# Transposed first-layer inputs kept in DRAM between two uses, in a fused state-space mixer and MLP

## The chip, the cores and the metric

The kernel runs on one core of a Trainium2 chip. The metric is device time in microseconds (us), the median of five runs. A profile, which is one execution taken by the hardware profiler, gives the times of the single instructions.

## The reference

```python
def _A_ref(x, Lambda_re, Lambda_im, B_re, B_im, C_re, C_im, log_dt, Dskip):
    Lam = Lambda_re + 1j * Lambda_im
    ...
    dt = jnp.exp(log_dt)
    Lam_bar = jnp.exp(dt * Lam)
    B_bar = ((Lam_bar - 1.0) / Lam)[:, None] * Bmat
    Bu = jnp.einsum("bld,pd->blp", x + 0j, B_bar)
    ...
    for t in range(L):
        h = Lam_bar[None, :] * h + Bu[:, t, :]
        hs.append(h)
    hseq = jnp.stack(hs, 1)
    return 2.0 * jnp.einsum("blp,dp->bld", hseq, Cmat).real + x * Dskip[None, None, :]

def _B_ref(x, w1, b1, w2, b2):
    y = _layernorm(x, axis=-1)
    h = _gelu(jnp.einsum("bsd,df->bsf", y, w1) + b1)
    return jnp.einsum("bsf,fd->bsd", h, w2) + b2

x = A_x
g = _sigmoid((x * gate_w).sum(-1, keepdims=True))
a = _A_ref(x, A_Lambda_re, ..., A_Dskip)
b = _B_ref(x, B_w1, B_b1, B_w2, B_b2)
return g * a + (1 - g) * b
```

x has 2048 tokens of 1024 channels in bfloat16, the state space has 1024 complex states, and the hidden layer of the MLP has 3584 columns.

## The kernel before

Every large product is done with seven block products instead of eight (Strassen's scheme in Winograd's form, class `SG`): a 2x2 split of both factors, four sums of the stationary blocks (S1 to S4) and four of the moving blocks (T1 to T4), and seven calls p1 to p7, each a run of matmuls with 512 moving columns recorded by the helper `mm` (line 839 where a bank is begun, line 841 where it is added to). Sums of blocks are VectorE subtractions and additions by the helper `dve_tt`, all with line 893.

The program runs through these stages on TensorE: the input product of the state space (the u blocks), then the list

```python
blocks = [("m", 0, 0), ("b", 0, 0), ("m", 0, 1), ("b", 0, 1), ("m", 1, 1), ("b", 1, 1), ("m", 1, 0), ("b", 1, 0), ("y", 0, 0)]
```

Here m(Fh, c) is the first MLP layer for half Fh of the hidden columns and half c of the tokens (c = 0 is the first 1024), seven groups of 256 hidden columns; b(Fh, c) is the second layer for the same halves, four groups of 256 tokens; y is the output product of the state space, eight groups. In m the moving factor is the transposed normalised x, which lies in an SBUF region `XN` of seven tiles, 128 partitions by 2048 two-byte values (512 KB) each. Tiles 0, 1 and 2 hold B11, B21 and B22; tiles 3, 4 and 5 hold T1, T2 and T3; tile 6 first holds B12, and T4 overwrites it. There is one such region, so m(0,0) uses the first tokens, m(0,1) and m(1,1) the second, and m(1,0) the first again.

`xn_load(c, q)` fills tiles 0, 6, 1 and 2 with four transposing DMAs (line 1217) from `scr_xn`, the normalised rows in DRAM, and `xn_sums` makes the other four tiles' contents with four subtractions of 2048 columns on VectorE, in the two later cases during the third group of the b block before the m block. Both happen three times: for c = 0 ahead of m(0,0), for c = 1 in b(0,0) and for c = 0 once more in b(1,1). The region is overwritten in place, so a load waits for the matmuls that last read its tile.

The state-space recurrence is VectorE work of sixteen units (`ssm`): load of u from `scr_u` (line 1147, on SP), multiplications and combinations (lines 1160 and 1163), scans (line 1174), and a store of the states to `scr_h` from POOL (line 1192). It runs between the sums and the evictions of the MLP stages: `cadd` (line 1297) in m, line 1379 in b. The first-layer weights come by line 1248 (raw, with four sums of 512 columns on VectorE after them, and kept in DRAM by line 1263 for the second hidden half) or by line 1245 (with their sums, from `scr_w1`). The second-layer weights come by line 1320, four pieces in the first groups of m(0,0) and of m(1,1), followed by four sums of 3584 columns. Second-layer results go to `scr_ac` from POOL (line 1386, and line 1388 adding in DRAM).

The order on each engine is not written by hand. Every operation is a task of class `Graph`, with a modelled duration, a priority and dependencies drawn from the buffers that it reads and writes. `_schedule_once` runs a list schedule of all tasks, and `emit` writes each engine's instructions in that fixed order with the semaphore waits. In a priority tuple the smaller goes first: MLP work has 10.0 and a position in TensorE's sequence (`q`), the recurrence has 50.0 and fills in. A DMA that follows another waits for it on the issuing engine, and an engine takes its list strictly in order. `extra` adds dependencies; `pe_last` is the matmul run that was recorded last. Plain and transposing loads are issued by SP, stores by POOL:

```python
def dma(self, prio, emit, nbytes, sem, reads=(), writes=(), name="", xpose=False, extra=(), ndma=1, bw=None, thr=False, q="sp"):
    if bw is None:
        bw = DMAT_BW if xpose else DMA_BW
    idur = {"sp": SP_ISSUE, "act": ACT_ISSUE, "pool": POOL_ISSUE}[q] * ndma
    ...
```

The main loop takes the groups in order; in iteration x of an m block it records p7 of the group before, p5, p6, p2 and p3 of this one, and then p4 of the group before.

Of the kernel before, what the change touches and what calls it, by code (L numbers as in the profile page):

```python
# [8 lines left out]
BF16 = mybir.dt.bfloat16  # L9
# [410 lines left out]
def build(nc, A_x, A_Lambda_re, A_Lambda_im, A_B_re, A_B_im, A_C_re, A_C_im, A_log_dt, A_Dskip,  # L420
          B_x, B_w1, B_b1, B_w2, B_b2, gate_w, out, stats=None):
# [22 lines left out]
    g = Graph()  # L444
    es = ExitStack()
    with es:
# [25 lines left out]
        AR = Arena(sb("ar", [128, ASZ // 2], BF16), ASZ)  # L472
# [7 lines left out]
        XN = AR.alloc(28672)  # L480
# [17 lines left out]
        B = g.buf  # L498
# [21 lines left out]
        def ssem(name, k, final=False):  # L520
            key = (name, k)
            if key not in slot_sems:
                slot_sems[key] = sem("d_%s%d" % (name, k), dram=final)
                if final and name in ("out", "outl"):
                    final_sems.append(slot_sems[key])
            return slot_sems[key]
# [57 lines left out]
        def bcast(ap, off, name):  # L584
# [11 lines left out]
              reads=[b_ones], writes=[b_ident], name="ident")  # L596
# [88 lines left out]
        def last_pe():  # L685
# [11 lines left out]
              reads=[b_stg, b_ident], writes=[b_ps[bk0]], name="cst_T", extra=last_pe())  # L697
# [3 lines left out]
              reads=[b_ones], writes=[b_stg], name="signs").slack = 4.0  # L701
# [3 lines left out]
              reads=[b_ps[bk0]], writes=[bc(n) for n in stage_names] + [b_ps[bk0]], name="cst_copy")  # L705
# [80 lines left out]
        for k in range(LT):  # L786
            n = 1 << k
# [15 lines left out]
        for p0 in range(0, PT, 4):  # L803
# [4 lines left out]
                  reads=[e1i], writes=[vt], name="tab_s%d" % p0)  # L808
# [16 lines left out]
        seq = [0]  # L825
        pb = [1.0]
        pe_last = []
# [380 lines left out]
            return AR.v(XN + i * 4096 + dt * 1024, [(1, 512)], FP16 if i > 2 else BF16)  # L1208


        def xn_load(c, q):
            for th in range(2):
                for dh in range(2):
                    i = (0, 1)[dh] if th == 0 else (6, 2)[dh]
                    o = AR.v(XN + i * 4096, [(512, 4), (1, 512)])
                    r0 = c * 1024 + th * 512
                    g.dma((10.0, q - 30, dh), lambda e, o=o, r0=r0, dh=dh: e.dma_start_transpose(out=o.ap, in_=XNS[r0:r0 + 512, dh * 512:(dh + 1) * 512]), 512 * 512 * 2,
                          ssem("xnT", i), reads=[b_xns[r0 // 128 + k] for k in range(4)], writes=[o], name="xnT%d.%d.%d" % (c, th, dh), xpose=True)
            xs_todo.append(c)
# [219 lines left out]
        def y_load(yi, ts=(0, 1), state=True):  # L1439

            qb = YORD[yi]
            o = AR.v(H0[yi], [(1, 2 * UE)])
            if state:
                g.dma((52.0, yi), lambda e: e.dma_start(out=o.ap, in_=HS[qb]), 2 * UE * 128 * 2, ssem("hg", yi), reads=[b_hs[pg][qb] for pg in range(PG)], writes=[o], name="hg%d" % yi,
                  extra=pe_last if yi > 2 else ())
            if yi == 0 and state:
                g.dma((51.0, 0), lambda e: e.dma_start(out=v_db.ap, in_=bass.AP(A_Dskip.tensor, A_Dskip.offset, [[0, 128], [1, D]])), 128 * D * 2, sem("d_dskb"), writes=[v_db], name="dskb")
            for t in ts:
                n = 2 * yi + t
                k = 2 * qb + t  # L1450
                av = AR.v(AV[n % 8], [(1, D)], F32)
                xi = 0 if n < 1 else 1 + n % 4
                xv = AR.v(XV[xi], [(1, D)])
                g.dma((52.0, n), lambda e, av=av, k=k: e.dma_start(out=av.ap, in_=ACS[k]), 128 * D * 4, ssem("yac", n % 8), reads=[b_acs[k]], writes=[av], name="acl%d" % k)
                g.dma((52.0, n), lambda e, xv=xv, k=k: e.dma_start(out=xv.ap, in_=x2[k * 128:(k + 1) * 128, :]), 128 * D * 2, ssem("yx", xi), writes=[xv], name="yx%d" % k)
                g.add("dve", c_tt16(D), (49.0, n), lambda e, xv=xv: e.tensor_tensor(xv.ap, xv.ap, v_db.ap, ALU.mult), reads=[xv, v_db], writes=[xv], name="xd%d" % k)
                g.add("dve", c_dve(D), (49.0, n, 1), lambda e, xv=xv, av=av, k=k: e.scalar_tensor_tensor(av.ap, xv.ap, C("G", k), av.ap, ALU.mult, ALU.add),
                      reads=[xv, av, bc("G")], writes=[av], name="xa%d" % k)
# [72 lines left out]
        for n, it in enumerate(flat):  # L1531
            bi, x = it
            kind, Fh, c = blocks[bi]
            last_of_block = (n + 1 == len(flat)) or flat[n + 1][0] != bi
            nit = None if n + 1 == len(flat) else flat[n + 1]
            if (kind, Fh, c, x) == ("b", 1, 0, 3):
                y_load(0, ())
            if (kind, x) == ("y", 0):
                y_load(2)
            if cur is None:  # L1540
                cur = make(it)
                cur.p1()

            if prev is not None:
                prev.p7()
            if kind == "b" and x + 1 < 4:
                prep_s((bi, x + 1), seq[0] + 4)
            if kind == "b" and Fh == 1 and c == 0 and x == 3:
                y_prep(0, seq[0] + 4)
            if kind == "y":  # L1550
                if x + 1 < 8:
                    y_prep(x + 1, seq[0] + 4)
            if kind == "b" and x == 0:

                cur.p2()
            if not early5:
                cur.p5()
            early5 = False
            cur.p6()
            if kind != "b" or x > 0:  # L1560
                cur.p2()
            if nit is None:
                cur.p7()
            cur.p3()
            if prev is not None:
                prev.p4()
                if kind == "y" and 1 <= x and x + 2 < 8:
                    y_load(x + 2)
                if kind == "m":
                    w2_step(seq[0] + 19)  # L1570
                if kind == "m" and 0 < x < 4:
                    w1_next(18)
                elif kind == "m":
                    w1_due[0] += x > 0
            if kind == "b":
                if w1_due[0]:
                    w1_due[0] -= 1
                    w1_next(20, list(pe_last))
                if x == XSG:
                    xn_sums(seq[0] + 20)  # L1580
            if n == 0:
                def em_b2(e):
                    return [e.dma_start(out=AR.v(B2B, [(1, D)], npart=1).ap, in_=bass.AP(B_b2.tensor, B_b2.offset, [[0, 1], [1, D]])),
                            e.dma_start(out=AR.v(B2B + 1024, [(1, 512)], npart=1, p0=1).ap, in_=bass.AP(B_b2.tensor, B_b2.offset, [[0, 1], [1, 512]]))]
                g.add("pool", 0.8, (39.0, 0), lambda e: e.memset(v_b2.ap, 0.0), writes=[v_b2], name="b2z")
                g.dma((40.0, 0), em_b2, 4096, sem("d_b2b"), writes=[v_b2l, v_b2r], name="b2b", ndma=2)
                w2_load(0)
                for pg in range(PG):
                    for q in range(NQ):
                        ssm(pg, q)  # L1590
            prev, cur = cur, pend
            pend = None
            if last_of_block:
                if nit is None:
                    prev.p4()
                else:
                    nk = blocks[nit[0]][0]
                    if nk == "b":
                        prep = True
                        b0 = None  # L1600

                        cur = make(nit)
                        prev.p7()
                        cur.p1()
                        prev.p4()
                        w1_due[0] += 1
                        prep_s(nit, seq[0])
                        pend = make((nit[0], nit[1] + 1))
                        pend.p1()
                    else:  # L1610
                        cur = make(nit)
                        prev.p7()
                        cur.p1()
                        cur.p5()
                        early5 = True
                        prev.p4()
                        if nk == "y":
                            y_load(0, (0, 1), False)
                            y_load(1)
                    prev = None  # L1620
                if (kind, Fh, c) == ("m", 1, 0):
                    ct_load(seq[0] + 20)

                if kind == "m":
                    if (Fh, c) == (0, 0):
                        xn_load(1, seq[0] + 20)
                    elif (Fh, c) == (1, 1):
                        xn_load(0, seq[0] + 20)
                elif (Fh, c) == (0, 1):
                    w2_load(1)  # L1630

# [42 lines left out]
```

## Time and profile before

| | |
|---|---|
| median of five runs | 568.03 us (565.0 to 570.68) |
| profiled execution | 566.27 us |
| its span, first to last instruction | 564.5 us |
| granted TensorE clock, mean | 0.996 |
| TensorE matmul busy | 548.5 us (97%), 2569 matmuls |
| VectorE busy | 519.8 us (92%) |
| ScalarE busy | 279.4 us (50%) |
| POOL busy | 96.3 us (17%) |
| DMA traffic | 125.32 MB, mean 222 GB/s |
| transposing loads from `scr_xn` (line 1217) | 12, median 5.4 us from issue to landing |
| stores to `scr_h` (line 1192), 512 KB each | 16, median 5.6 us, 2.9 to 12.3 |

The span starts with the first instruction, and all positions in time count from there. Busy time is the time in which an engine ran compute instructions; issuing a DMA is not counted as busy for SP. "DMA share" in a window is the mean busy share of the core's 16 DMA engines (it can read a little over 1.00 at the edges of a window). In a list of waits, a line names the engine that stood still, its tile and line, then the instruction that released it, the sum of such waits, their number and the longest.

### The profile page before, as it was taken

How to read it: one execution, taken by the hardware profiler on the slowest of the kernel's cores; microseconds unless marked ns; L12 is line 12 of the kernel's file. 1: busy time of each engine (PE TensorE's matmuls, PEld its weight loads, DVE VectorE, ACT ScalarE, POOL GpSimd, SP SyncE). 2: the span in 40 equal slices, each digit the busy share in tenths (PEclk: the TensorE clock that was granted, in tenths of full speed). 3: DMA queues.
4: the chain of work that ended last, by engine and by line, in shares of the span. 5: the costliest groups of instructions: out<-in, count | busy, mean ns of one | idle time of the engine just before them, and what ended most of it. 6: DMA issues, size and time to landing. Idle time of an engine off the chain costs nothing.

```text
span 564.5 us, 7433 instructions
## 1 busy us (share of the span) xinstructions
PE 548.5 (97%) x2569; PEld 251.7 (45%) x2617; DVE 519.8 (92%) x893; ACT 279.4 (50%) x465; POOL 96.3 (17%) x155
## 2 busy tenths in 40 slices
PE   6999999999999999999989999999999999999995
PEld 5444444444444444444434444444444444444442
DVE  4899999999999999999999999999998995999852
ACT  3969989677652346752236763246763231111110
POOL 0226736620001110001110101220001210000100
PEclk9999999999999999999999999999999999999998
DMA  9995999749774463305988895999778699978501
GB/s 280 237 310 133 284 299 270 262 130 295 218 157 162 175 224 111 113 37 164 322 322 296 287 326 148 228 200 268 261 179 188 114 304 348 393 258 297 188 37 56
DMA packets 122035, 125.32 MB, mean 222 GB/s; under 512 B 70532, under 2 KB 99717, under 8 KB 120974
## 3 DMA queue, kind: packets, MB, share of 16 engines
q1 hardware_dynamic: 108852, 76.97, 47.9%
q0 software_dynamic: 13008, 47.87, 27.1%
q8 instruction: 20, 0.33, 0.2%
q14 instruction: 17, 0.14, 0.1%
q10 hardware_dynamic: 138, 0.02, 0.0%
HBM read 60.73 MB, written 48.38 MB: 193 GB/s over the span
## 4 chain that ended last, share of the span: by engine, by line
PE 82%; DVE 11%; issue 2%; DMA 2%; ACT 1%; POOL 0%; SPq 0%; DVEq 0%
PE ps L841 56%; PE ps L839 25%; DVE ar L893 2%; DVE ar L1174 2%; DMA scr_u<-ar 1%; DVE ar L1160 1%; DVE ar L1019 1%; DVE ar L979 1%; DVE ar L974 1%; PE ps L665 1%; DMA ar<-in_A_B_re_dram 1%; PE ps L1044 1%; DVE ar L820 1%; DVE ar L822 0%; DVE ar L1163 0%
## 5 line engine op out<-in xcount | busy, mean ns | idle before, releaser
L841 PE MATMUL ps<-ar 128*128 128x512 f16 (+1 forms) x1684 | 390.4, 379 | 4.3 <-DVE ar L1379 1.4
L841 PEld LDWEIGHTS ps<-ar 128*128 128x128 f16 (+1 forms) x1720 | 167.7, 98 | 207.0 <-DVE ar L1379 1.9
L839 PE MATMUL ps<-ar 128*128 128x512 bf16 (+1 forms) x744 | 182.8, 380 | 0.6 <-DVE cst L704 0.3
L893 DVE TENSOR_TENSOR ar<-ar 128x512 f16<-128x512 bf16 (+7 forms) x244 | 150.9, 652 | 3.4 <-ACT ar L669 1.0
L839 PEld LDWEIGHTS ps<-ar 128*128 128x128 bf16 (+1 forms) x752 | 73.3, 98 | 89.0 <-issue 1.6
L1174 DVE TENSOR_TENSOR_SCAN ar<-cst,init,ar 128x256 bf16<-128x256 f32 x128 | 88.1, 733 | 0.3
L857 ACT ACTIVATE ar<-ps 128x512 f32<-128x512 f32 x100 | 58.8, 593 | 49.4 <-PE ps L839 34.0
L1160 DVE TENSOR_TENSOR ar<-ar 128x2048 bf16<-128x2048 bf16 x64 | 77.2, 1216 | 0.0
L865 ACT ACTIVATE ps<-ps 128x512 f32<-128x512 f32 x66 | 38.5, 583 | 71.1 <-PE ps L839 71.0
L1293 ACT ACTIVATE ar<-ps,cst 128x512 bf16<-128x512 f32 x56 | 38.4, 686 | 26.7 <-PE ps L841 25.9
L858 ACT ACTIVATE ar<-ps,cst 128x512 f32<-128x512 f32 x32 | 22.0, 687 | 53.4 <-PE ps L839 27.2
L1376 ACT ACTIVATE ar<-ps,cst 128x512 f32<-128x512 f32 x32 | 22.0, 687 | 46.8 <-PE ps L841 46.8
L1163 DVE TENSOR_TENSOR ar<-ar 128x1024 bf16<-128x1024 bf16 x64 | 42.6, 685 | 0.3
L1299 ACT ACTIVATE ar<-ar,cst 128x512 bf16<-128x512 f32 x56 | 40.0, 714 | 5.5 <-DVE ar L1297 5.4
L1297 DVE TENSOR_TENSOR ar<-ps,ar 128x512 f32<-128x512 f32 x56 | 38.3, 684 | 2.8 <-PE ps L841 2.5
L908 POOL DMA_DIRECT2D scr_u<-ar x32 | 24.9, 780 | 35.3 <-DVE ar L974 21.4
L1388 POOL DMA_DIRECT2D scr_ac<-ar x16 | 13.8, 875 | 97.9 <-DVE ar L1379 49.3
L1478 DVE SCALAR_TENSOR_TENSOR ar<-ps,cst,ar 128x512 bf16<-128x512 f32 x32 | 23.5, 745 | 7.1 <-PE ps L841 6.9
L1379 DVE SCALAR_TENSOR_TENSOR ar<-ps,cst,ar 128x512 f32<-128x512 f32 x32 | 23.8, 744 | 2.5 <-PE ps L841 2.2
L1192 POOL DMA_DIRECT2D scr_h<-ar x16 | 9.7, 605 | 91.4 <-DVE ar L1163 91.4
L1386 POOL DMA_DIRECT2D scr_ac<-ar x16 | 8.5, 532 | 90.3 <-DVE ar L893 48.0
L1485 POOL DMA_DIRECT2D out_dram<-ar x14 | 7.6, 543 | 83.8 <-DVE ar L1478 83.5
(106 smaller groups left out, 257.4 us busy)
## 6 DMA issues: line engine op xcount, KB each, us to landing
scr_ac<-ar POOLq DMA_DIRECT2D x32, 512.0 KB, 5.9
ar<-in_B_w_dram SPq DMA_DIRECT2D x21, 512.0 KB, 5.4
ar<-in_A_x_dram SPq DMA_DIRECT2D x32, 256.0 KB, 5.6
scr_u<-ar POOLq DMA_DIRECT2D x32, 256.0 KB, 4.4
ar<-scr_u SPq DMA_DIRECT2D x16, 512.0 KB, 4.9
scr_h<-ar POOLq DMA_DIRECT2D x16, 512.0 KB, 5.6
ar<-scr_h SPq DMA_DIRECT2D x8, 1024.0 KB, 5.9
ar<-scr_ac SPq DMA_DIRECT2D x16, 512.0 KB, 7.5
```

The lines of the kernel that those rows point to most:

```text
L839: ins = e.matmul(V(PS[bk], 0, [(1, n)]), st[i].ap, mv[i].ap, start=(i == 0), stop=(i == K - 1))
L841: ins = e.matmul(V(PS[bk], 0, [(1, n)]), st[i].ap, mv[i].ap, start=False, stop=(i == K - 1), skip_group_check=True)
L857: return e.activation(o.ap, V(PS[bk], 0, [(1, 512)]), AF.Copy)
L865: g.add("act", c_act(512), (pb[0], q - 2), lambda e: e.activation(V(PS[b], 0, [(1, 512)]), V(PS[a], 0, [(1, 512)]), AF.Copy), reads=[b_ps[ ...
L893: g.add("dve", c_tt16(n), (pb[0], q), lambda e: e.tensor_tensor(o.ap, a.ap, b.ap, op), reads=[a, b], writes=[o], name=nm, extra=ex).slack ...
L908: g.dma((1.0, q), lambda e: e.dma_start(out=US[pt // 4, :, 4 * pr:4 * pr + 4, r0:r0 + T], in_=evv.ap), 2 * 128 * CH * 2, ssem("us", 2 * ks ...
L1160: g.add("dve", c_tt16(UE), pri(i), lambda e: e.tensor_tensor(o.ap, a.ap, tbl.ap, ALU.mult), reads=[a, tbl], writes=[o], name=nm + tag)
L1163: g.add("dve", c_tt16(UE // 2), pri(i), lambda e: e.tensor_tensor(o.ap, a.ap, b.ap, op), reads=[a, b], writes=[o], name=nm + tag)
L1174: lambda e, pt=pt, ri=ri, vin=vin, go=go: e.tensor_tensor_scan(go.ap, Cb("R", pt, T), vin.ap, V(INIT, pt * 2 + ri, [(1, 1)]), ALU.mult, AL ...
L1293: g.add("act", c_act(512, ap_operands=1), (10.0, q + 1), lambda e: e.activation(o.ap, V(PS[bk], 0, [(1, 512)]), AF.Gelu_apprx_tanh, bias=C ...
L1297: g.add("dve", c_dve(512), (10.0, q - 2), lambda e: e.tensor_tensor(sv.ap, V(PS[bk], 0, [(1, 512)]), sv.ap, ALU.add), reads=[b_ps[bk], sv] ...
L1299: g.add("act", c_act(512, psum=False, ap_operands=1), (10.0, q + 3), lambda e: e.activation(o.ap, sv.ap, AF.Gelu_apprx_tanh, bias=C("B1", ...
```

## The change

Two helpers are added. `xn_keep` stores one of the seven tiles into a new DRAM tensor `scr_xnq` from POOL, not before the matmul run given as `extra`. `xn_again` loads the seven tiles back from SP, in the order XQO. In m(0,0) the iterations x = 3, 4 and 5 store two tiles each and x = 6 stores the last one (tiles 0 and 3, 4 and 1, 5 and 2, and 6). After m(1,1) `xn_again` takes the place of the third `xn_load`; it enters nothing into `xs_todo`, so the four sums in b(1,1) are not made.

```diff
+        XNQ = nc.dram_tensor("scr_xnq", (128, 7 * 2048), BF16, kind="Internal").ap()
+        b_xnq = [B("xnq%d" % i) for i in range(7)]
+
+        XQO = (0, 3, 4, 1, 5, 2, 6)
+
+        def xn_keep(i, q, ex):
+            o = AR.v(XN + i * 4096, [(1, 2048)])
+            g.dma((10.0, q), lambda e: e.dma_start(out=XNQ[:, i * 2048:(i + 1) * 2048], in_=o.ap), 128 * 4096,
+                  ssem("xnk", i, True), reads=[o], writes=[b_xnq[i]], name="xnk%d" % i, q="pool", extra=ex)
+
+        def xn_again(q):
+            for n, i in enumerate(XQO):
+                o = AR.v(XN + i * 4096, [(1, 2048)])
+                g.dma((10.0, q - 30, n), lambda e, o=o, i=i: e.dma_start(out=o.ap, in_=XNQ[:, i * 2048:(i + 1) * 2048]), 128 * 4096,
+                      ssem("xnT", i), reads=[b_xnq[i]], writes=[o], name="xnl%d" % i)
...
+                if (kind, Fh, c) == ("m", 0, 0) and x >= 3:
+                    for i in XQO[2 * x - 6:2 * x - 4]:
+                        xn_keep(i, seq[0], list(pe_last))
                 if kind == "m":
                     w2_step(seq[0] + 19)
...
                     if (Fh, c) == (0, 0):
                         xn_load(1, seq[0] + 20)
                     elif (Fh, c) == (1, 1):
-                        xn_load(0, seq[0] + 20)
+                        xn_again(seq[0] + 20)
```

## The prediction

> **What bounds the kernel now.** I read the spans first: one core, 564.5 us, granted clock 0.996. The profiled execution took 566.27 us, so 1.77 us lie around its span, and it is 1.76 us below the median of the five runs, 568.03 us (565.0 to 570.68). About 1% (5.7 us) is what a measurement of this kernel can tell from no change.
>
> Next I cut the span into stages by the windows. Columns: TensorE (PE), weight load, VectorE (DVE), ScalarE and POOL busy, then clock, DMA share, GB/s.
>
> ```profile
> 136.00:162.00 26.00, 25.64 (x118) 11.40 (x118) 25.79 (x40) 17.80 (x30) 0.55 (x1) 1.00 0.82 229
> ...
> 289.00:332.00 43.00, 41.08 (x187) 18.46 (x190) 42.17 (x67) 27.76 (x46) 3.72 (x7) 1.00 0.93 327
> 332.00:375.00 43.00, 42.79 (x197) 19.46 (x199) 42.58 (x63) 15.24 (x23) 6.14 (x8) 1.00 0.85 193
> 375.00:418.00 43.00, 42.84 (x198) 19.51 (x200) 41.63 (x65) 28.80 (x48) 2.96 (x5) 1.00 0.90 254
> ...
> 461.00:540.00 79.00, 78.60 (x360) 35.61 (x366) 68.86 (x94) 13.12 (x22) 6.82 (x12) 1.00 0.81 282
> 540.00:564.50 24.50, 17.70 (x82) 7.84 (x80) 9.00 (x13) 1.78 (x3) 1.62 (x3) 0.92 0.15 54
> ```
>
> The blocks are found by their matmul counts: m(0,0) is 114 to 161, b(1,1) 332 to 375, m(1,0) 375 to 418. TensorE is busy in all but 0.1 to 0.4 us of each stage; only the stage of m(1,1) (289 to 332) loses 1.92 us. From 118 to 540 the sum of its idle time is 422.00 - 418.05 = 3.95 us. The rest of the 16.0 us that the span has over 548.5 us of matmul lies mostly in the first 10 us (4.45) and after 540 (6.80), where the change does nothing. VectorE is the second limit: 42.58 of 43.00 us in the very stage that the change relieves.
>
> Then the waits, those of TensorE alone:
>
> ```profile
> PE ps L649 <- DMA ar<-in_A_x_dram: 3.6, 1, 3.6
> PE ps L841 <- DVE ar L1379: 1.4, 1, 1.4
> PE ps L665 <- DMA ar<-in_A_B_re_dram: 0.7, 1, 0.7
> PE ps L841 <- DVE ar L893: 0.6, 2, 0.3
> PE ps L839 <- DVE cst L704: 0.3, 1, 0.3
> ```
>
> The three for DMA or the constants are in the start. Asked for 332 to 564 alone, the list is empty: TensorE waits for nobody from b(1,1) to the end. The chain that ended last says the same: 56% L841 and 25% L839, an almost unbroken run of matmuls from 123 us on. Full VectorE and full TensorE run side by side; TensorE sets the end.
>
> **What the change removes.** Four transposing loads and four sums, all in b(1,1):
>
> ```profile
> 327.12 12.55 SPq L1217 DMA_TRANSPOSE ar<-scr_xn  x4
> ```
>
> ```profile
> 363.06 3.49 DVE L893 TENSOR_TENSOR ar<-ar 128x2048 f16<-128x2048 bf16 x3
> ...
> 367.13 1.21 DVE L893 TENSOR_TENSOR ar<-ar 128x2048 f16<-128x2048 bf16 x1
> ```
>
> On VectorE that is 3.49 + 1.21 = 4.70 us. The transposes hold SP from 327.12 to 339.67; SP's next instruction is a weight load at 343.10, which waits for TensorE, so SP gains nothing that is awaited. The 4.70 us let the state-space units, which fill VectorE's gaps, end earlier. Who waits for them? TensorE's whole idle time from 332 to 540 is 208.00 - 207.03 = 0.97 us. So the relief is worth 0 to 0.97 us. I take 0, because the list of waits in that stretch is empty.
>
> **What it adds in b(1,1).** Seven plain loads of 512 KB from SP in place of four transposes: an issue of the like (L1147, 512 KB) holds SP 0.32 to 0.53 us, 7 x 0.43 = 3.0 us instead of 12.55. They move 7 x 524,288 = 3.67 MB, 1.57 MB more than the 2.10 MB of the transposes. At 207 GB/s, the slowest rate that this place shows (337 to 342), they need 17.7 us. The order of loading is the order of last use, and the last tile is free when p4 of the last m group ends, at 335.3. All are there by 335.3 + 17.7 = 353; the first matmul on them comes at about 374. Cost 0; the cover is 21 us of second-layer matmuls, and without it each late us would be an us of the end. Behind them on SP stands the weight load of 343.10 (5.5 us to land), for a block that starts 25 us later.
>
> **What it adds in m(0,0).** Seven stores of 512 KB on POOL, each pair held until p4 of the group before has run: by TensorE's timeline at 138.7, 144.7 and 151.2 us, the last single one at 157.2. Issuing costs POOL 0.55 us as for this row:
>
> ```profile
> 149.03 0.55 POOL L1192 DMA_DIRECT2D scr_h<-ar  x1 [22.04 <-DVE ar L1163]
> ```
>
> That is 7 x 0.55 = 3.9 us on an engine busy 0.55 of 26 us. POOL takes its list in order, so the state store (L1192) may stand behind a held pair. SP's reload of that buffer (L1147 at 159.83) waits for it, and for that VectorE at 183.6 at the earliest; the reload landed at 164.7, so 18.9 us are spare.
>
> The traffic is the real price. Seven stores need 8.8 us of all DMA engines at 416 GB/s (326 to 332, the fullest of the short windows), or 17.3 us at 212 GB/s, the mean of this stage. What is free:
>
> ```profile
> 139.00:142.00 3.00, 3.00 (x16) 1.36 (x14) 2.97 (x6) 2.19 (x5) 0.00 (x0) 1.00 1.00 327
> 142.00:145.00 3.00, 2.95 (x15) 1.35 (x15) 3.00 (x4) 1.93 (x5) 0.00 (x0) 1.00 0.96 284
> 145.00:149.00 4.00, 3.75 (x18) 1.52 (x17) 3.86 (x9) 3.22 (x6) 0.00 (x0) 1.00 0.77 239
> 149.00:152.00 3.00, 3.00 (x15) 1.37 (x14) 3.00 (x5) 1.69 (x4) 0.55 (x1) 1.00 0.44 179
> 152.00:157.00 5.00, 4.95 (x24) 2.17 (x23) 5.00 (x6) 3.56 (x7) 0.00 (x0) 1.00 0.47 105
> 157.00:162.00 5.00, 5.00 (x25) 2.27 (x24) 5.00 (x8) 3.29 (x5) 0.00 (x0) 1.00 1.14 232
> 162.00:170.00 8.00, 7.95 (x38) 3.62 (x37) 8.00 (x14) 2.64 (x4) 0.00 (x0) 1.00 0.50 117
> ```
>
> By the DMA share: 0 + 0.12 + 0.92 + 1.68 + 2.65 + 0 + 4.00 = 9.4 us free to 170 us. So other transfers come later by nothing (8.8 < 9.4) up to 17.3 - 9.4 = 7.9 us. What is late then, and what it can bear:
> - The first-layer weights of group 6, issued 139.35, landed after 6.6 us at 145.95; VectorE sums them from 151.5. Spare: 5.6 us. This is the tightest.
> - The last second-layer piece, issued 144.9, landed 149.9; its sum on VectorE is the single 128x3584 one after 160.3. Spare: 10.4 us.
> - The next transposes (L1217) now wait for the stores as well. The fourth, at 160.99, overwrites the tile stored last. With a landing of 5.6 us (the median for L1192) from 157.2 the store is done at 162.8, with the longest, 12.3, at 169.5. The transpose landed at 166.6 and is read by VectorE at 189.3: 22.7 us spare against a delay of 1.8 to 8.5. On SP behind it stands the weight load of 169.03: SP is free again 3.65 us (that transpose's own issue) after the store, at 166.5 or at worst at 173.2. That is 4.2 us late; the load then lands within 5.6 us (the longest of the three there) at 178.8, before its sums at 179.6.
>
> So the cost here is 0 at one end. At the other, 7.9 us less 5.6 spare is 2.3 us on VectorE, which is full and gives them on to TensorE. I take 0: the first 1.05 MB, the only stores ahead of the group-6 weights, need 2.5 us at 416 and 4.9 at 212 GB/s, both under 5.6.
>
> A rule that speaks against stores on POOL: the Trainium skill, "DMA: Bandwidth & Descriptors", section "SWDGE vs HWDGE vs iDMA", says that descriptors made by GpSimd can be starved while VectorE holds their shared path in its two-port modes, and SP's transfers are immune. Here POOL's rows issue in 0.53 to 0.87 us beside a VectorE 97 to 99% busy, so the trace shows no starving. The same page ("Anatomy of one DMA") prices such a transfer at 2.0 us plus bytes over 436 GB/s, by which one store would be an estimated 3.2 us; the measured 5.6 decides, and by either the sum stays 0.
>
> **What the planner moves.** The order on each engine is written ahead from modelled costs. New tasks in the plan shift it from 138 us on, and the missing sums shift VectorE's after 332. No row prices that. Below, it cannot win more than the 3.95 us of idle time; above, I take as many again. I take 0, with both ends for the range.
>
> **Sum.** 0 - 0 (to 0.97) + 0 (to 2.3) + 0 (-3.95 to +3.95): span 564.5, its execution 566.3, on the median 568.0 us.
>
> **Rivals.**
> (1) *The stores delay the weights of m(0,0).* Price: in full 7.9 us, 568.0 + 7.9 = 575.9. It decides from the point where the group-6 weights land after their sums are due: as the order stands, when the stores run below 3.67 MB / (9.4 + 5.6 us) = 245 GB/s; the full price falls due if the new order also eats the 5.6 us spare. For it: share 1.00 at 139 us, VectorE busy 25.79 of 26 us and so unable to catch up, and TensorE already waiting twice 0.3 us for such sums (L893). Against it: the stage goes idle from 149 to 157, and the first pair alone does not fill the spare time.
> (2) *The rewritten order costs waits.* One more such wait as at 291 us (1.4) up to the whole 3.95: 568.0 + 4.0 = 572.0. For it: VectorE has 0.4 us of room per stage, so a misplaced sum shows at once. Against it: the planner's stages hold TensorE to within 0.4 us everywhere but once.
> (3) *VectorE's relief reaches TensorE.* It ends the 0.97 us and, by a luckier order, the 1.92 us of m(1,1): 568.0 - 2.9 = 565.1. For it: VectorE is 99% busy in b(1,1). Against it: no wait of TensorE lies after 332.
> (4) *The loads do not come back in time,* so m(1,0) waits. The 21 us above would have to go; under 0.02, and at 80 GB/s (46 us for 3.67 MB) it would cost 335.3 + 46 - 374 = 7 us: 575.
>
> **Chances.** Forecast 0.60, (1) 0.12, (2) 0.15, (3) 0.11, (4) 0.02. Slower by over 1%: (1), (4) and a sixth of (2), 0.16. Faster by over 1% needs more than the idle time that can be reached and rests on scatter of the runs: 0.03 out of (3). Within 1%: 0.81. The range runs from the forecast less 3.95 us with half a us rounded off, 564.5, to the end of (2) with the 1.5 us that the median may scatter upwards, 573.5.
>
> **What would show it.** Right: no L1217 after 300 us, seven short SP issues near 326 to 336, no 128x2048 f16 sums on VectorE near 365, seven more POOL stores from 139 to 158, TensorE's list of waits still empty after 332, its idle time from 118 to 540 near 4 us, the last state store (460.0) some 4 us earlier. Wrong: a TensorE wait for L893 near 147 to 160 us (rival 1), new waits for L1379, L1297 or L893 elsewhere (rival 2), a TensorE wait for DMA near 375 (rival 4), or a lower clock.

## The result, and the profile after

The changed kernel takes 570.17 us in the median (53 runs, 568.06 to 583.83) against 567.82 us before (95 runs, 564.85 to 578.93). The ratio is 1.0043, 95% interval 1.0028 to 1.0058. It is slower, by 2.4 us (1.6 to 3.3 by the interval). The profiled execution took 572.43 us with a span of 570.7, so it is one of the longer ones; a second profile was taken later (569.5 us of span). Executions more than 1.5% above the fastest of their kernel count in the medians and ranges but not in the ratios.

The same windows as before, of the changed kernel. Columns: TensorE, weight load, VectorE, ScalarE, POOL busy, clock, DMA share, GB/s.

```profile
136.00:162.00 26.00, 23.89 (x108) 10.44 (x109) 25.76 (x41) 16.61 (x27) 4.24 (x8) 1.00 1.05 299
...
289.00:332.00 43.00, 42.08 (x192) 18.86 (x195) 40.61 (x65) 27.49 (x46) 4.40 (x9) 1.00 0.98 341
332.00:375.00 43.00, 42.27 (x194) 19.08 (x196) 42.74 (x67) 15.45 (x24) 6.30 (x8) 1.00 0.82 230
375.00:418.00 43.00, 42.79 (x197) 19.46 (x199) 39.71 (x62) 27.82 (x47) 3.34 (x5) 1.00 0.92 258
...
461.00:540.00 79.00, 75.52 (x339) 33.84 (x344) 66.68 (x91) 11.93 (x20) 7.05 (x13) 0.98 0.82 278
```

TensorE's idle time is the window less its busy time. It grew by 1.75 us in m(0,0) (2.11 against 0.36), by 0.52 in b(1,1) and by 3.08 at the y stage (3.48 against 0.40), and it shrank by 1.00 in m(1,1) (0.92 against 1.92). The list of TensorE's waits names the same places; the waits of the start, for x, B and constants, are left out:

```profile
PE ps L841 <- DVE ar L1494: 3.2, 1, 3.2
PE ps L839 <- DVE ar L893: 1.5, 1, 1.5
PE ps L841 <- DVE ar L1395: 0.7, 1, 0.7
PE ps L841 <- DVE ar L1313: 0.6, 1, 0.6
PE ps L841 <- DVE ar L893: 0.5, 2, 0.3
```

L1494 and L1395 are the evictions of y and b (1478 and 1379 before), L1313 is `cadd` (1297 before), L893 the sums. A wait after 332 us, where there was none, is now the longest of them. It cost more than the 3.2 us for which TensorE stood still:

```profile
483.96 3.36 PE L841 MATMUL ps<-ar 128*128 128x512 f16 x8 [3.17 <-DVE ar L1494]
```

The eight matmuls behind the wait took 3.36 us, where eight take 1.90 elsewhere; the granted clock reads 0.50 from 484 to 486 us. This is 1.46 us more, which no idle time shows. The second profile has no such stretch.

After 540 us TensorE is idle for 7.43 us (7.45 in the second profile) against 6.80 before. That lies behind the last store: from the issue of the last store of the output to the end of the span 6.5 us pass, 5.9 before.

What the change set out to do it did. The chain on SP in b(1,1) shows plain loads (L1224) where transposes stood, seven in 9.59 us, each landing within 8.1 us:

```profile
327.16 9.59 SPq L1224 DMA_DIRECT2D ar<-scr_xnq  x7
344.02 30.62 SPq L1261 DMA_DIRECT2D ar<-scr_w  x4
```

No sum of 2048 columns stands near 365 us any more, and VectorE's busy time in all fell from 519.8 to 514.8 us.

### The profile page after: what moved, and what is told of

It is laid out like the page before. It is cut to its first block, busy times and chain, and to the rows that moved or that the text cites. A ratio compares the mean times of both kernels' runs of the same rounds, so it can differ in the third digit from the quotient of the medians.

```text
span 570.7 us, 7458 instructions
## 1 busy us (share of the span) xinstructions
PE 549.9 (96%) x2569; PEld 251.4 (44%) x2617; DVE 514.8 (90%) x889; ACT 279.4 (49%) x465; POOL 99.9 (18%) x162
## 4 chain that ended last, share of the span: by engine, by line
PE 79%; DVE 11%; DMA 6%; issue 2%; ACT 0%; SPq 0%; DVEq 0%
PE ps L841 54%; PE ps L839 24%; DMA ar<-in_A_x_dram 3%; DVE ar L893 3%; DMA ar<-in_B_w_dram 2%; DVE ar L1174 2%; DVE ar L1160 1%; DVE ar L1163 1%; DVE ar L1313 1%; PE ps L665 1%; DMA ar<-in_A_B_re_dram 1%; DVE ar L979 1%; PE ps L1044 1%; DVE ar L1019 1%; DVE ar L974 0%
## 5 line engine op out<-in xcount | busy, mean ns | idle before, releaser
L893 DVE TENSOR_TENSOR ar<-ar 128x512 f16<-128x512 bf16 (+7 forms) x240 | 145.7, 642 | 6.7 <-ACT ar L1315 1.9
L865 ACT ACTIVATE ps<-ps 128x512 f32<-128x512 f32 x66 | 38.5, 583 | 75.4 <-PE ps L839 75.3
L1313 DVE TENSOR_TENSOR ar<-ps,ar 128x512 f32<-128x512 f32 x56 | 38.1, 681 | 3.8 <-PE ps L841 3.5
L1473 DVE SCALAR_TENSOR_TENSOR ar<-ar,cst 128x1024 f32<-128x1024 bf16 x16 | 20.3, 1274 | 10.6 <-DMA ar<-scr_ac 10.6
L1494 DVE SCALAR_TENSOR_TENSOR ar<-ps,cst,ar 128x512 bf16<-128x512 f32 x32 | 23.5, 743 | 7.0 <-PE ps L841 6.9
L1395 DVE SCALAR_TENSOR_TENSOR ar<-ps,cst,ar 128x512 f32<-128x512 f32 x32 | 23.7, 744 | 4.7 <-DMA scr_ac<-ar 3.0
L1192 POOL DMA_DIRECT2D scr_h<-ar x16 | 9.4, 587 | 86.3 <-DVE ar L1163 86.3
```

The lines of the kernel that those rows point to most:

```text
L865: g.add("act", c_act(512), (pb[0], q - 2), lambda e: e.activation(V(PS[b], 0, [(1, 512)]), V(PS[a], 0, [(1, 512)]), AF.Copy), reads=[b_ps[ ...
L893: g.add("dve", c_tt16(n), (pb[0], q), lambda e: e.tensor_tensor(o.ap, a.ap, b.ap, op), reads=[a, b], writes=[o], name=nm, extra=ex).slack ...
L1313: g.add("dve", c_dve(512), (10.0, q - 2), lambda e: e.tensor_tensor(sv.ap, V(PS[bk], 0, [(1, 512)]), sv.ap, ALU.add), reads=[b_ps[bk], sv] ...
```

## The experiments

**Where each place is read.** The run times of all kernels scatter by several us. The profiles show one source of it ahead of the change: in some executions VectorE waits near 74 us for a transposing load of B, and TensorE loses 2.6 to 5.5 us between 60 and 118 us (the profiles of e2, e6, e7, e8 and e9). No edit here alters VectorE's order that early, and it differs between executions of one kernel: e7 and e10 are the same program and lost 5.54 and 0.17 us there. So I read the causes stage by stage from the profiles and give the ratios with their intervals beside them. Most of the profiles lack some matmul records (2569 against 2617), which shows as about 0.2 us of idle time per stage; the last two, with 2617, show 0 there. The windows are fixed while the stages shift with the losses ahead of them, so a wait can straddle an edge: in e10 the wait of 1.44 us that belongs to m(1,1) begins before 289, and its 0.94 stands for 1.8 us; in e6 0.3 us of m(0,0) fall behind 162.

TensorE's idle time in us, by window, with the ratio to the kernel before, run on the same chip:

| kernel | 136-162 | 289-332 | 332-375 | 461-540 | ratio, 95% interval |
|---|---|---|---|---|---|
| before | 0.36 | 1.92 | 0.21 | 0.40 | |
| the change | 2.11 | 0.92 | 0.73 | 3.48 | 1.0043, 1.0028 to 1.0058 |
| the change, second profile | 2.11 | 0.92 | 0.65 | 1.84 | 1.0083, 1.0049 to 1.0118 |
| e1: stores, old reload with sums | 2.02 | 0.86 | 0.16 | 0.52 | 0.9970, 0.9937 to 1.0003 |
| e2: plain reload, no stores, no sums | 0.45 | 1.85 | 0.21 | 2.02 | 0.9983, 0.9953 to 1.0014 |
| e3: before less the four sums | 0.36 | 1.83 | 0.21 | 2.31 | 1.0034, 1.0000 to 1.0069 |
| e5: change, planner sees small stores | 0.36 | 1.99 | 0.21 | 2.32 | 1.0003, 0.9971 to 1.0035 |
| e6: change, two y loads held | 1.84 | 0.87 | 0.21 | 0.32 | 1.0028, 0.9991 to 1.0066 |
| e7: e5 and e6 together | 0.41 | 1.93 | 0.21 | 0.32 | 1.0023, 0.9980 to 1.0067 |
| e8: before, two y loads held | 0.45 | 1.97 | 0.21 | 0.32 | 1.0014, 0.9979 to 1.0049 |
| e9: e6 with the stores moved | 1.12 | 1.32 | 0 | 0 | 1.0008, 0.9973 to 1.0043 |
| e10: e7 once more | 0.25 | 0.94 | 0 | 0.60 | 0.9975, 0.9942 to 1.0009 |

**The changed kernel, profiled once more.**

> The change unaltered, for a second profile on this chip: idle time of TensorE of 2.0 us from 136 to 162 and of 2 to 3.5 us from 461 to 540 if both waits belong to the program and not to one execution; 2.4 us slower than before.

The idle time of m(0,0) is 2.11 us again. The y stage idled 1.84 us, under the range expected. The stage is the same, the waits in it are not:

```profile
PE ps L839 <- DVE ar L893: 2.8, 3, 1.5
PE ps L841 <- DVE ar L1494: 0.2, 1, 0.2
```

Of the three waits for sums, that of 1.5 us is the one in m(0,0). The other two, 1.4 us together, are sums of states at 500 and 513 us, in the y stage, and the eviction L1494 cost only 0.2. So the size of the loss, and the instruction that pays it, differ from execution to execution. The ratio is 1.0083.

**e1, the stores alone.** After m(1,1) the old transposing loads and sums are back.

```diff
                     elif (Fh, c) == (1, 1):
-                        xn_again(seq[0] + 20)
+                        xn_load(0, seq[0] + 20)
```

> The seven stores of m(0,0) stay; after m(1,1) the old way is back: four transposing loads and four sums. Theory (two separate costs: a TensorE wait in m(0,0), where the profile of the changed kernel has 2.1 us of idle time from 136 to 162 us against 0.4 before, and a wait of 3.2 us at the entry of the y stage, which not every run need show): only the first is left, so about 1.5 us slower than before, with one TensorE wait for L893 of about 1.5 us near 153 us and none after 332. Rival 1 (the stores are the whole loss): 2.4 us slower, like the changed kernel. Rival 2 (the loss is at the y stage alone): no difference.

The wait of 1.5 us for L893 in m(0,0) is there, and the y stage is as before. But the idle time of m(1,1) fell by 1.06 us as well, so the stages give +1.66 - 1.06 + 0.12 = +0.7 us instead of the 1.5 that I had expected, and the ratio, 0.997, does not show even that. The expected time was a miss: I had forgotten that the gain in m(1,1) comes with the stores. As a place the first cost is confirmed, and the y stage is cleared of the stores. In this profile TensorE also waited 1.5 us for ScalarE's seed (L865) between 118 and 136, which e2, e7 and e8 have too, with and without stores.

**e2, the plain reload without stores,** from rows that lie in DRAM anyway (so the last first-layer block has other inputs).

```diff
-                if (kind, Fh, c) == ("m", 0, 0) and x >= 3:
-                    for i in XQO[2 * x - 6:2 * x - 4]:
-                        xn_keep(i, seq[0], list(pe_last))
...
-e.dma_start(out=o.ap, in_=XNQ[:, i * 2048:(i + 1) * 2048])
+e.dma_start(out=o.ap, in_=XNS[i * 256:(i + 1) * 256, :].rearrange("(p r) d -> p (r d)", r=2))
```

> No stores; seven plain loads of 512 KB after m(1,1) as in the change, but from the normalised rows that lie in DRAM anyway, so the values of the last first-layer block are others; the four sums are left out. Theory: no wait in m(0,0), a wait at the y stage of 1 to 3 us, so 0.5 to 2 us slower than before. Rival 1 (stores are the whole loss): no difference, or up to 0.9 us faster. Rival 2 (y stage alone): 2.4 us slower.

**e3, the sums alone left out,** with the transposing loads kept.

```diff
                         xn_load(0, seq[0] + 20)
+                        xs_todo.pop()
```

> The kernel before with nothing but the four sums of b(1,1) left out (the last first-layer block then multiplies with stale tiles); the transposing loads stay. VectorE's order is the same as without stores and with plain loads. If the y stage suffers because the missing sums let the planner issue loads of the y stage in another order, it is as slow as the run with plain loads and no stores, 0.5 to 2 us slower than before, with VectorE waiting 10 us for a load of scr_ac near 465 to 475. If the plain loads are at fault, it is as fast as before or faster by up to 0.9 us.

Both keep the 0.4 us of m(0,0) and both lose 2.0 to 2.3 us at the y stage, e3 with the old loads. So the plain reload is not at fault; what suffices is that the sums are gone. The windows of e3 for m(0,0) and the y stage show it in their TensorE column, 25.64 and 76.69:

```profile
136.00:162.00 26.00, 25.64 (x118) 11.36 (x119) 25.80 (x40) 17.87 (x30) 0.55 (x1) 1.00 0.82 230
...
461.00:540.00 79.00, 76.69 (x348) 34.09 (x353) 66.70 (x91) 12.87 (x22) 6.86 (x12) 1.00 0.83 284
```

In e2 TensorE waited there 1.1 us for a load of states (`scr_h`), 0.4 for their sums and 0.2 for an eviction, in e3 0.6 us for each of the three. The times (0.9983 and 1.0034) straddle 1 and settle nothing.

**e5, the planner does not see the stores.** The stores move what they moved, at the same points; only the size given to the planner is another.

```diff
-            g.dma((10.0, q), lambda e: e.dma_start(out=XNQ[:, i * 2048:(i + 1) * 2048], in_=o.ap), 128 * 4096,
+            g.dma((10.0, q), lambda e: e.dma_start(out=XNQ[:, i * 2048:(i + 1) * 2048], in_=o.ap), 128 * 4,
```

> The whole change, with the same stores at the same points, but the planner is told that a store moves 512 bytes instead of 512 KB, so it does not push other work back for them: VectorE's order in m(0,0) is that of the kernel before. If the order is what costs in m(0,0) (the planner put the sums of the group-6 weights 2 us later, behind state-space work; the load itself landed at 150.0, before the old place of its sums at 151.5), the TensorE wait of 1.5 us near 153 is gone and the time is that of the run with plain loads and no stores, 1.5 us below the changed kernel. If the traffic is what costs (the load took 11.4 us instead of 6.6), the wait stays at 1.5 us or more and the time is that of the changed kernel.

This tells traffic from order. In the change and in e5 the load of the group-6 weights (512 KB, L1264) took the same 11.4 us to land, against 6.6 before: the traffic is there in both, and it ate 4.8 of the 5.6 us that were spare. In the change the load was there at 150.0 us, and VectorE came to the sums at 153.4, behind state-space work. VectorE's timeline of the change:

```profile
150.20 0.68 DVE L1313 TENSOR_TENSOR ar<-ps,ar 128x512 f32<-128x512 f32 x1
150.80 1.28 DVE L1163 TENSOR_TENSOR ar<-ar 128x1024 bf16<-128x1024 bf16 x2
152.12 0.75 DVE L1174 TENSOR_TENSOR_SCAN ar<-cst,init,ar 128x256 bf16<-128x256 f32 x1
152.79 0.67 DVE L1313 TENSOR_TENSOR ar<-ps,ar 128x512 f32<-128x512 f32 x1
153.37 0.75 DVE L893 TENSOR_TENSOR ar<-ar 128x512 f16<-128x512 bf16 x2
```

and of e5, where the sums follow the eviction directly, and of the kernel before, with the same order:

```profile
150.56 0.68 DVE L1313 TENSOR_TENSOR ar<-ps,ar 128x512 f32<-128x512 f32 x1
151.16 3.02 DVE L893 TENSOR_TENSOR ar<-ar 128x512 f16<-128x512 bf16 x4
154.10 0.68 DVE L1313 TENSOR_TENSOR ar<-ps,ar 128x512 f32<-128x512 f32 x1
```

```profile
150.92 0.68 DVE L1297 TENSOR_TENSOR ar<-ps,ar 128x512 f32<-128x512 f32 x1
151.52 3.02 DVE L893 TENSOR_TENSOR ar<-ar 128x512 f16<-128x512 bf16 x4
154.46 0.68 DVE L1297 TENSOR_TENSOR ar<-ps,ar 128x512 f32<-128x512 f32 x1
```

In e5 there is no wait for these sums, and VectorE stood still in none of the three. So the 1.75 us of m(0,0) are the planner's. Its code counts a load at 0.55 of its speed while POOL's channel is busy. In the plan that the code computes, this load ends at 146.56 us in the kernel before and in e5 and at 148.84 in the change, and its sums begin at 150.11 and at 152.78. So two combinations and a scan of the state space, which in the other two kernels stand behind these sums, went in front of them, and TensorE stood still for the sums from 152.4 us. With the order of before, the 1.00 us won in m(1,1) is gone as well (1.99 in e5): that gain was a draw of the same order and not a fruit of the reload.

**e6, two loads of the y stage held.** The names in the planned order of SP show what the missing sums let loose. Loads of `scr_ac` (line 1470, 512 KB each; k is the token block) stood in this order: before, acl9, acl10, acl8, two loads of x, acl0, acl1; in the change, acl9, acl10, acl0, acl1, acl8, loads of x. The order of e2 and e3 is that of the change, the order of e1 that of before. The first y group needs acl8. Blocks 0 and 1 belong to the fourth group and go to slots that hold the state-space tables; the state space is done earlier without the sums (its last product on VectorE ends at 455.5 instead of 458.4), so these slots are free earlier and their loads go first.

```diff
-g.dma((52.0, n), ..., ssem("yac", n % 8), reads=[b_acs[k]], writes=[av], name="acl%d" % k)
+g.dma((52.0, n), ..., ssem("yac", n % 8), reads=[b_acs[k]], writes=[av], name="acl%d" % k, extra=pe_last if yi == 3 else ())
```

> The whole change, and one edit at the entry of the y stage: the two loads of scr_ac for the fourth y group (acl0, acl1, 512 KB each) get the last matmul run as an extra dependency, so SP issues them behind the loads of the second and third group instead of in front of the first group's own load. If these two loads, let go early because the sums are gone, cause the wait at the y stage, TensorE's idle time from 461 to 540 falls from 2 to 3.5 us to 0.5 or less and the kernel is 1.5 to 3 us faster than the change, about 0.6 us over before (the wait of 1.5 in m(0,0) stays, 1.0 less in m(1,1)). If the y stage waits because DMA is full there anyway, nothing moves.

The idle time of the y stage is 0.32 us; the wait in m(0,0) and the gain in m(1,1) stay, as expected. In time, too, the edit gains about what was expected: measured on the same chip, the change has a median of 573.88 us, e6 571.65 and e7, below, 572.00; the intervals of their ratios overlap, though. SP before, in the change, and then in e6:

```profile
451.87 4.80 SPq L1454 DMA_DIRECT2D ar<-scr_ac  x3
456.73 0.90 SPq L1455 DMA_DIRECT2D ar<-in_A_x_dram  x2
458.41 0.80 SPq L1454 DMA_DIRECT2D ar<-scr_ac  x2
```

```profile
452.77 5.23 SPq L1470 DMA_DIRECT2D ar<-scr_ac  x5
458.06 2.59 SPq L1471 DMA_DIRECT2D ar<-in_A_x_dram  x3
```

```profile
457.79 4.92 SPq L1470 DMA_DIRECT2D ar<-scr_ac  x3
462.75 2.93 SPq L1471 DMA_DIRECT2D ar<-in_A_x_dram  x3
```

And what VectorE waited for at this place in the change:

```profile
461.09 0.75 DVE L1395 SCALAR_TENSOR_TENSOR ar<-ps,cst,ar 128x512 f32<-128x512 f32 x1 [2.96 <-DMA scr_ac<-ar]
...
474.98 1.28 DVE L1473 SCALAR_TENSOR_TENSOR ar<-ar,cst 128x1024 f32<-128x1024 bf16 x1 [10.61 <-DMA ar<-scr_ac]
```

acl8 was issued at 457.7 and landed after 17.3 us, at 475.0, when L1473 starts; before, it was issued at 456.4 and landed after 6.0. In e6 it landed after 6.2 us. Behind L1473 in VectorE's list stood the evictions of the y groups and a wait of 1.3 us for x, and TensorE, which needs their PSUM banks again, waited 3.17 us, until 483.96, for L1494. In the other profiles with this order (the second one of the change, e2, e3, e5) acl8 landed after 12.1 to 14.5 us and VectorE waited 6.2 to 7.7 us for it; there TensorE met the delay later and in parts, at evictions, at sums of states and at a load of states. With the order of e6 all of these waits are gone from its profile. The DMA share is 1.0 from 452 to 482 in the kernel before and in the change alike; the order in the jam decides who is late.

**e7 and e10, both edits.**

> Both edits on the change: the planner sees the stores as 512 bytes, and the two loads of scr_ac are held. If the two waits are the whole loss, TensorE's idle time from 118 to 540 is that of before (4 us, 1.9 of it in m(1,1)) and the time equals before within 0.5 us. If the plain reload or the stores cost something else as well, 1 us or more is left.

> The run with both edits once more (the planner sees the stores as 512 bytes, the two loads of scr_ac held), for its time: its first interval, 0.998 to 1.0067, could tell it neither from before nor from the change, since the stages before 118 us, which no edit touches, lost up to 5.5 us in its profile. If the two waits are the whole loss, the ratio to before is 1.000 within 0.0035 and the idle time from 136 to 540 is 3.9 us as before.

In e7 the four stages are those of before within 0.1 us, with the reload, the stores and the missing sums all in place. From 136 to 540 us TensorE is idle 404.00 - 400.13 = 3.87 us, before 404.00 - 400.16 = 3.84. In e10 it is idle 2.63 us, less than the 3.9 expected because its profile holds all matmul records; all of it is waits. Those of the y stage are 0.6 us for a load of states (`scr_h`), which e7 does not have, and nothing for L1494. The ratios, 1.0023 and 0.9975, hold 1 between them; neither interval excludes it.

**e8, a control.** The edit of e6 on the kernel before.

> The kernel before with only the two loads of scr_ac held. Control: before shows 0.40 us of idle time from 461 to 540, so there is nothing to win in its profile; same time as before within 0.5 us. If it is faster than before by 1 us or more, the entry of the y stage costs before too, in runs that its one profile does not show.

No difference (1.0014), and nothing to win at the y stage (0.32 against 0.40).

**e9, the stores moved** to where the DMA engines stood idle before, with the edit of e6.

```diff
-                if (kind, Fh, c) == ("m", 0, 0) and x >= 3:
-                    for i in XQO[2 * x - 6:2 * x - 4]:
+                if (kind, Fh, c) == ("m", 0, 0) and x in (0, 5, 6):
+                    for i in {0: XQO[:3], 5: XQO[3:6], 6: XQO[6:]}[x]:
```

> The change with the two loads of scr_ac held, and with the stores where the DMA engines stood idle in the profile of before: three in x = 0 (from 120 us), three in x = 5 and one in x = 6; the planner sees their true size. If it is the planned order beside the stores that costs in m(0,0), a wait there is drawn anew: idle time from 136 to 162 of 0.4 us if no load of weights stands beside the stores in the plan, 1 to 2 us if one does. The y stage stays at 0.3 us. Time between 1 us under before and 1 us over.

The wait for L893 is 1.1 us instead of 1.5, and m(1,1) idles 1.32: another draw of the order, no better than before (1.0008). None of the versions is shown to beat the kernel before.

## Why the prediction was wrong, point by point

I forecast no difference; the kernel is slower by 0.43%, inside the range of times and under the 1% that I took for the limit of what can be told. More runs told it.

- *What bounds the kernel* held. TensorE sets the end, and 4.70 us less on VectorE won nothing in any profile.
- *The reload in b(1,1), cost 0,* held. The seven loads were landed by 336.4 + 8.1 = 344.5 us at the latest, earlier than the 353 that I allowed, and m(1,0) waited for none of them. They held SP for 9.59 us, not the 3.0 that I had put, at no cost.
- *The stores, "0 at one end, 2.3 us at the other"*: the traffic cost 0, as taken. The tightest spare time was named rightly and almost used up (4.8 of 5.6 us), and e5 shows that it sufficed. Rival 1 gave the right place and the right wait, L893 near 153 us, by the wrong mechanism: not the late load but a plan that expected it later still.
- *What the planner moves, "I take 0, with both ends"* is the first term that failed. It was +1.75 us in m(0,0) and -1.00 in m(1,1), +0.7 together. I wrote that no row prices it. One did: TensorE's wait of 0.3 us for the sums in m(0,0) said that these are made just in time, so a plan that moves them back by 1.9 us costs about that. (Rival 1 put both of the waits of 0.3 us in m(0,0); one of them is at 322 us, in m(1,1).) The factor 0.55 with which the plan slows SP beside POOL stands in the code.
- *The relief, "worth 0 to 0.97 us", with 0 taken,* is the second and larger one; its range had the wrong sign. I asked who waits for the state space and found nobody. I did not ask what its earlier end sets free: table slots, and through them two loads of 512 KB that go ahead of an urgent one into a stage where the DMA share reads 1.0. It cost 1.44 and 3.08 us of idle time in the two profiles of the change, 1.6 to 1.9 in e2, e3 and e5. The execution with 3.08 paid 1.46 us more for a halved clock; I had named a lower clock as a sign of being wrong, without a price. No rival named it; rival 2 (the rewritten order) covers its kind but looked for it in VectorE's order, not in SP's. The sign that I gave for the relief did not come either: the last product of the state space ended 2.9 us earlier, but its store (L1192) was issued at 460.3, not some 4 us ahead of 460.0, since two stores to `scr_ac` stood before it in POOL's list.
- *"after 540 (6.80), where the change does nothing,"* was wrong by about 0.6 us. All eight profiles with the stores idle 7.3 to 7.5 us there, the four without them 6.8 to 6.9. The cause was not tested; the stores bring seven semaphores more.

The sum of idle time: +0.7 for the plan in m(0,0) and m(1,1), 1.4 to 3.1 at the y stage, 0.4 to 0.5 in b(1,1), 0.6 at the end, 3.3 to 5.0 us in the two profiles, against 2.4 us (1.6 to 3.3) by the runs. The lower one just fits. The higher belongs to the execution of 572.43 us, and with the 1.46 us of the slow clock its 6.4 us account for the 6.2 us by which that span is longer than the one before.

Open: the 0.4 to 0.5 us of b(1,1). In both profiles of the change VectorE waited 1.4 to 1.6 us near 326 for a load of weights (`in_B_w`, 512 KB) that landed after 11.1 and 10.9 us; in e6, with the same VectorE order up to the y stage, it landed after 8.3 and nobody waited. Why it is slower in the change stays open. Open too is the time of the single edits: intervals of some 0.35% to each side are as wide as the effects, and the separation rests on the profiles, one for each kernel, two for the change and for both edits together.

## What to carry to other kernels

Work taken off an engine that is not the bound is not free of consequence: follow what its earlier end releases, slot by slot and queue by queue, above all loads that then pass a more urgent one in an in-order queue. Where a planner writes the order ahead, give a new transfer's modelled size as much care as its place: here the same traffic cost 1.75 us in its stage with one modelled size (0.7 net of what the same plan won elsewhere) and nothing with another. Tie loads that are wanted late to something late, so that they cannot go early.

## What the runs showed of the hardware

In a stage where the DMA share is 1.0, the time to land of one and the same 512 KB load went from 6.0 to 17.3 us with two other loads of 512 KB issued 1.8 to 2.2 us ahead of it (12.1 to 14.5 in the four other profiles with this order). In m(0,0), 1.05 MB of stores from POOL beside it took a 512 KB weight load from 6.6 to 11.4 us, 4.8 us longer, where I had put the stores at 2.5 to 4.9 us.

After TensorE's wait of 3.17 us the granted clock read 0.50 for 3.4 us, and eight matmuls of 512 columns took 597 ns in the mean instead of the usual 379. Waits of 2.65 us (e6) and 2.43 us (e9) near 78 us were followed by the same, one of 3.25 us (e8) was not.
